# Left-over 64-token blocks of linear attention: two heads on a zero-filled 128x128 block, one full-array product

## The chip, the cores and the metric

The kernel runs on one core of a Trainium2 chip. The metric is the device time of one execution in microseconds (us), as a median over repeated runs. Profiles come from one profiled execution. TensorE is called PE, its weight loads PEld, VectorE DVE, ScalarE ACT, GpSimd POOL, and SyncE SP; SP issues the transfers.

## The reference

Linear attention with random features is followed by two dense feed-forward layers on the same tokens. Everything is float32.

```python
batch, n_heads, seq, head_dim = (4, 8, 576, 64)          # 128 features
q_s, k_s = (q * scale, k * scale)
def phi(x):
    proj = np.einsum('bhsd,md->bhsm', x, omega)           # 64 -> 128
    h = proj - np.sum(x * x, axis=-1, keepdims=True) / 2.0
    return np.exp(h - np.max(h, axis=-1, keepdims=True)) / np.sqrt(m)
kv = np.einsum('bhsm,bhsd->bhmd', phi(k_s), v)
num = np.einsum('bhsm,bhmd->bhsd', phi(q_s), kv)
den = np.einsum('bhsm,bhm->bhs', phi(q_s), np.sum(phi(k_s), axis=2))[..., None] + 1e-06
x = (num / den)                                           # as (2304, 512)
x = leaky(x @ moe_w_in, 0.01) @ moe_w_out                 # 512 -> 2048 -> 512
h = x @ moe2_w_in
out = (h * clip(h + 3, 0, 6) / 6) @ moe2_w_out            # 512 -> 2048 -> 512
```

## The kernel before

Heads are held in pairs: partitions 0 to 63 of a tile are one head's 64 features, partitions 64 to 127 the other's. A sequence of 576 tokens is four blocks of 128 tokens and one left-over block of 64. The function `scores` projects a unit's blocks with `omega` (the tile `wn`, which holds omega twice, once for each half of the partitions). The stationary operand of each product is a token block from the tile `xT`, the moving operand is 64 rows of `wn` with 128 columns. So one product uses half of PE's rows, and two of them, one for each head of the pair, form a couple on the two halves. For a left-over block the 64 tokens of head 0 go to partitions 0 to 63 of a bank and those of head 1 to partitions 64 to 127 of the same bank; such a product uses a quarter of the array, 64 rows by 64 columns. These products stand on line 753 (units of queries and of keys) and on line 774 (`K_tail`: the left-over keys of all four head pairs of a batch at once).

After the products `features` takes minima on DVE (L719), adjusts them (L722, L724), and takes exponentials on ACT (L729). A key unit then multiplies with the values (L822), transposes (L829) and sums keys (L846). A query unit forms its denominators on DVE (L922, reciprocal L928), scales on POOL or DVE (L933), transposes on PE (L948) and multiplies with `kvf` (L979).

`PARTS` cuts each batch's queries into units for five groups of tokens: an entry (group, f, half) has f full blocks and, if half is true, a left-over block. There are three shapes with a left-over block: `half` alone (one unit with four head pairs in batch 0 and one in batch 3), f=1 with half (two units of two head pairs, batch 1), and f=3 with half (four units of one head pair, batch 2).

The first dense layer (`moe1`) runs in products on full-array tiles on lines 502 to 504, three for each float32 product split in a high and a low part. Its weights are unpacked from 64-bit numbers and split on DVE, ACT and POOL (L532 to L552, L486, L487) while it runs, in the first 160 us. The attention of a group is laid among the products of the dense layer of the group before it. The second layer (lines 1076 and 1176) fills the rest of the time.

The order of every engine's work comes from a planner, `Graph.run`, which runs before the kernel is built. It keeps a clock for each engine, takes costs from the code (`"pe", nh * (f + half) * 224.0`), and always issues the operation that can start first. For attention work on PE it has a mode: "S" for products on halves of the rows (scores), "N" for products on halves of the columns (L822, L979), "F" for full-array float32 work, "M" for the dense layers. `WAIT` holds an operation of a mode back if PE last ran "M", so that work of one mode gathers, and `TURN` is the planner's price of a change of mode. So an edit to a cost or a mode can move any attention operation.

Of the kernel before, what the change touches and what calls it, by code (L numbers as in the profile page):

```python
# [19 lines left out]
B, H, S, D = 4, 8, 576, 64  # L20
# [17 lines left out]
PACE = 2.215  # L38
WAIT = {"S": 4500.0, "N": 2000.0, "F": 1500.0}
FOLLOW = 500.0  # L40
# [313 lines left out]
def attn_moe_kernel(ctx: ExitStack, tc: tile.TileContext, qT, kT, qn, kn, v1, om2, w1i, w1o, w2i, w2o, out):  # L354
# [378 lines left out]
    def scores(f, half, xsrc, nsrc, due, nh=1):  # L733

        cols, before = layout(f, half, nh)
        one = f * 128 + 64 * half
        ntok = nh * one
        sq = squares(sum(cols), nsrc, due, nh)
        src = Buf("xT")
        to = lambda: src.tiles[0][:, 0:ntok]  # L740
        g.op(dma((lambda: to().rearrange("p (h t) -> p h t", h=nh)) if nh > 1 else to, xsrc, 128 * ntok * 4), wr=[src], due=due - O2)
        ps = [Ps(g.use) for _ in cols]
        hs = [Buf("h" if c > 1 else "hh") for c in cols]

# [12 lines left out]
        features(ps, hs, cols, before, sq, due, nh)  # L757
        return hs, cols
# [3 lines left out]
    def K_tail(b, due):  # L762
# [3 lines left out]
        last64[b] = h  # L766
        g.op(dma(lambda: src.tiles[0][:, 0:HP * 64].rearrange("p (h t) -> p h t", h=HP), kT[b, :, :, 512:576].rearrange(
            "h p t -> p h t"), 128 * HP * 256), wr=[src], due=due - O2)

        def mm():  # L770
            for hp in range(HP):
                for e in range(2):
                    r = slice(64 * e, 64 * e + 64)
                    nc.tensor.matmul(p.tiles[0][r, hp * 128:hp * 128 + 128], lhsT=src.tiles[0][r, hp * 64:hp * 64 + 64], rhs=wn[r],
                                     start=True, stop=True)
# [123 lines left out]
    def Q_unit(grp, b, hps, f, half, s0, col0, o, due):  # L899
        n, nh = f * 128 + 64 * half, len(hps)  # L900
        ncol, N, F = 2 * f + half, nh * n, f * 128
        if nh == 1:
            xsrc, nsrc = qT[b, hps[0], :, s0:s0 + n], qn[b, hps[0], :, col0:col0 + ncol]
        else:
            h0, h1 = hps[0], hps[-1] + 1
            xsrc = qT[b, h0:h1, :, s0:s0 + n].rearrange("h p t -> p h t")
            nsrc = qn[b, h0:h1, :, col0:col0 + ncol].rearrange("h p c d -> p h c d")
# [373 lines left out]
    for b in range(B):  # L1281
        s0 = col0 = 0
        for i, (grp, f, half) in enumerate(PARTS[b]):
            o = b * S + s0 - GT[grp]
            many_ = min(HP, 4 // max(1, f + half)) if grp else 1
            part = [[("Q", b, list(range(k, k + many_)), f, half, s0, col0, o)] for k in range(0, HP, many_)]
# [4 lines left out]
            s0, col0 = s0 + f * 128 + 64 * half, col0 + 2 * f + half  # L1291
    wi1, wo1 = [], []
# [157 lines left out]
```

## Time and profile before

| | |
|---|---|
| median of 3 runs | 869.18 us (868.69 to 870.06) |
| profiled execution, its own time | 870.25 us |
| span of the profile | 868.4 us |
| PE busy | 855.1 us (98%) |
| DVE busy | 661.5 us (76%) |
| ACT busy | 511.7 us (59%) |
| POOL busy | 197.1 us (23%) |
| transfers | 192.76 MB, mean 222 GB/s |

The span reaches from the first to the last recorded instruction; 1.85 us of the execution lie outside of it. Busy time of PE is that of overlapping products, whose ends are modelled, so the cost of a PE operation is read from the start of one row to the start of the next. A float32 product appears as two records, a transpose as one.

### The profile page before, as it was taken

Reading aid. Unit: us, or ns where it says so; the run is one execution under the profiler, and the core shown is the slowest. Engines: PE = TensorE matmul, PEld = TensorE weight load, DVE = VectorE, ACT = ScalarE, POOL = GpSimd, SP = SyncE. Lnnn points to the kernel's source line nnn. Section 1 sums busy time; section 2 is a strip of 40 time slices with the busy share of each in tenths; the row PEclk is TensorE's granted clock in tenths of the full one; section 3 lists DMA queues with packets and bytes.
Section 4 is the critical chain, followed back from the end, with each engine's and each line's share of the span. In section 5 each row is a group of like instructions: output and inputs, shape, how many; then the busy total and the mean of one; then the engine's idle time right before and its main releaser. Section 6 shows DMA issues by size and latency. Waiting matters only on the chain.

```text
span 868.4 us, 17807 instructions
## 1 busy us (share of the span) xinstructions
PE 855.1 (98%) x6340; PEld 776.5 (89%) x6340; DVE 661.5 (76%) x1714; ACT 511.7 (59%) x1162; POOL 197.1 (23%) x289
## 2 busy tenths in 40 slices
PE   9999999999999999999999999999999999999998
PEld 8988777889877877888888889999999999999997
DVE  6998988966996773666778747796678779868765
ACT  6987887976688654544565445544543454345442
POOL 0124363432314231010101002131002213322110
PEclk9999999999999999999999999999999999999999
DMA  9565654677367504998788718877896784687451
GB/s 334 173 189 184 194 186 141 207 249 219 120 215 251 172 25 161 339 356 331 271 290 319 260 49 301 271 297 248 279 318 216 235 269 136 220 269 246 134 163 45
DMA packets 88616, 192.76 MB, mean 222 GB/s; under 512 B 14416, under 2 KB 40656, under 8 KB 88528
## 3 DMA queue, kind: packets, MB, share of 16 engines
q1 hardware_dynamic: 88528, 191.63, 65.6%
q8 instruction: 50, 0.82, 0.4%
q14 instruction: 38, 0.31, 0.1%
HBM read 147.55 MB, written 44.04 MB: 221 GB/s over the span
## 4 chain that ended last, share of the span: by engine, by line
PE 81%; DVE 12%; DMA 3%; ACT 2%; issue 1%; POOL 0%; SPq 0%; DVEq 0%
PE bank L1076 18%; PE bank L1176 16%; PE bank L502 13%; PE bank L503 12%; PE bank L504 12%; PE bank L753 3%; DVE junk L922 2%; DMA late_w<-in 1%; PE bank L822 1%; PE bank L979 1%; DVE wt L545 1%; DVE wst L542 1%; DVE w L486 1%; DVE nm L719 1%; PE bank L948 1%
## 5 line engine op out<-in xcount | busy, mean ns | idle before, releaser
L483 ACT COPY late_u<-bank 128x256 f32<-128x256 f32 (+1 forms) x100 | 38.4, 384 | 83.8 <-PE bank L1176 70.8
L1018 DVE TENSOR_TENSOR g<-bank,g 128x512 fp32r<-128x512 f32 (+1 forms) x80 | 50.7, 634 | 44.3 <-ACT g L483 43.7
L1076 PE MATMUL bank<-w,g 128*128 128x256 f32 x606 | 80.9, 276 | 0.5 <-DVE g L486 0.5
L1076 PEld LDWEIGHTS bank<-w,g 128*128 128x128 f32 x606 | 74.1, 192 | 0.9 <-DVE g L486 0.7
L1016 ACT ACTIVATE bank<-bank 128x512 f32<-128x512 f32 (+1 forms) x80 | 44.2, 553 | 50.7 <-PE bank L504 50.5
L1176 PE MATMUL bank<-x,late_w 128*128 128x256 f32 x564 | 70.8, 275 | 0.8 <-DMA late_w<-in 0.7
L1176 PE MATMUL bank<-w,late_w 128*128 128x256 f32 x534 | 71.4, 276 | 0.1
L729 ACT ACTIVATE h<-bank,nm 128x128 f32<-128x128 f32 x228 | 64.4, 384 | 6.4 <-DVE nm L724 5.8
L1176 PEld LDWEIGHTS bank<-x,late_w 128*128 128x128 f32 x564 | 67.0, 192 | 1.3 <-DVE late_xr L490 0.9
L502 PE MATMUL bank<-g,w 128*128 128x512 f32 (+1 forms) x180 | 67.4, 375 | 0.2 <-DVE g L1018 0.2
L502 PE MATMUL bank<-x,w 128*128 128x512 f32 (+1 forms) x180 | 66.9, 372 | 0.0
L1176 PEld LDWEIGHTS bank<-w,late_w 128*128 128x128 f32 x534 | 65.6, 192 | 0.6 <-DMA late_w<-in 0.3
L504 PE MATMUL bank<-x,w 128*128 128x512 f32 (+1 forms) x180 | 64.6, 359 | 1.0 <-DVE x L486 1.0
L504 PE MATMUL bank<-g,w 128*128 128x512 f32 (+1 forms) x180 | 64.7, 359 | 0.1
L503 PE MATMUL bank<-x,w 128*128 128x512 f32 (+1 forms) x180 | 64.5, 358 | 0.0
L503 PE MATMUL bank<-g,w 128*128 128x512 f32 (+1 forms) x180 | 64.5, 358 | 0.0
L719 DVE TENSOR_REDUCE nm<-bank 128x4 f32<-128x512 f32 (+2 forms) x76 | 47.5, 653 | 14.7 <-PE bank L753 13.3
L1076 PE MATMUL bank<-second_w,g 128*128 128x256 f32 x423 | 56.6, 275 | 0.0
L933 POOL TENSOR_TENSOR h<-h,den 128x512 f32<-128x512 f32 (+2 forms) x32 | 33.5, 1051 | 85.1 <-DVE den L928 53.8
L1076 PEld LDWEIGHTS bank<-second_w,g 128*128 128x128 f32 x423 | 51.9, 192 | 0.0
L483 ACT COPY u<-bank 128x256 f32<-128x256 f32 (+1 forms) x52 | 21.6, 415 | 43.6 <-PE bank L1176 31.4
L922 DVE CUSTOM_DVE_ANT_0 junk<-h,zr 128x128 bf16<-128x128 f32 (+1 forms) x128 | 44.7, 386 | 1.7 <-ACT h L729 0.7
(388 smaller groups left out, 2365.2 us busy)
## 6 DMA issues: line engine op xcount, KB each, us to landing
late_w<-in SPq DMA_DIRECT2D x85, 512.0 KB, 4.6
in<-late_w SPq DMA_DIRECT2D x32, 512.0 KB, 5.2
late_w<-in SPq DMA_DIRECT2D x39, 256.0 KB, 4.8
third_w<-in SPq DMA_DIRECT2D x19, 512.0 KB, 4.7
wst<-w2i SPq DMA_DIRECT2D x16, 512.0 KB, 4.4
wst<-w2o SPq DMA_DIRECT2D x16, 512.0 KB, 4.9
x_t<-late_w SPq DMA_DIRECT2D x12, 512.0 KB, 4.9
v<-v SPq DMA_DIRECT2D x14, 330.0 KB, 4.0
```

The source lines that it names most:

```text
L483: return [("act", c_act(n, psum), lambda: nc.scalar.copy(dst(), src())), dve if psum else dve + (True,)]
L502: nc.tensor.matmul(o, lhsT=ah, rhs=bh, start=start, stop=False)
L503: nc.tensor.matmul(o, lhsT=al, rhs=bh, start=False, stop=False)
L504: nc.tensor.matmul(o, lhsT=ah, rhs=bl, start=False, stop=stop)
L719: g.op([("dve", c_dve(c * 128), lambda raw=raw, n_=n_: nc.vector.tensor_reduce(out=n_()[:, :, 0], in_=raw(), axis=AX.X, op=ALU.min))], rd= ...
L729: nc.scalar.activation(h.tiles[0][:, q * 128:q * 128 + 128], raw()[:, q], AF.Exp, bias=nm.tiles[0][:, q], scale=-1.0)
L922: nc.vector.tensor_tensor_reduce(out=jk.tiles[0][r, q % 2], in0=h.tiles[0][r, q * 128:q * 128 + 128], in1=zr[k].tiles[0][r, e], scale=1.0, ...
L933: eng.tensor_tensor(out=x, in0=x, in1=den.tiles[1][:, 0:c].to_broadcast([128, c, 128]), op=ALU.mult)
L1016: g.op([("act", c_act(n, True), lambda: nc.scalar.activation(P(), P(), AF.Prelu, alpha=0.01))], wr=[p], due=d)
L1018: g.op([("dve", c_dve(n), lambda: nc.vector.tensor_tensor(out=G1(), in0=P(), in1=G0().bitcast(F32), op=ALU.subtract))], rd=[p, (gg, 0)], w ...
L1076: nc.tensor.matmul(acc[bank].tiles[0][:, half * 256:half * 256 + 256], lhsT=src.tiles[x][:, q * 128:q * 128 + 128], rhs=woven(w[k].tiles[y ...
L1176: nc.tensor.matmul(R[r](), lhsT=w[x], rhs=m[y], start=start and k == n == 0, stop=k == 1 and n == 2, skip_group_check=True)
```

## The change

Left-over blocks of two heads are laid out as one 128x128 block: the 64 tokens of head 0 take the first 64 columns on partitions 0 to 63, those of head 1 the last 64 columns on partitions 64 to 127, and the other two quarters are zeros. The host fills in the zeros, so `qT` and `kT` have 640 columns instead of 576. One product with all 128 rows of `wn` then gives the same bank contents as the two products before. `scores` issues these full-array products first and then the couples on halves; for `half` alone the unit has no couple left and its mode is "F". `K_tail` does the same for batches 1, 2 and 3; batch 0 keeps its two products. The left-over blocks cost 112 instead of 224 in the planner, and the wait for mode "F" is 1100 instead of 1500. Line numbers of the changed kernel after `K_tail` are 5 higher.

```diff
-WAIT = {"S": 4500.0, "N": 2000.0, "F": 1500.0}
+WAIT = {"S": 4500.0, "N": 2000.0, "F": 1100.0}
...
-        one = f * 128 + 64 * half
+        one = (f + half) * 128
...
         def mm():
+            for k in range(nh if half else 0):
+                at = (k * (f + 1) + f) * 128
+                nc.tensor.matmul(ps[0].tiles[0][:, at:at + 128], lhsT=src.tiles[0][:, at:at + 128], rhs=wn, start=True, stop=True)
             for k in range(nh):
-                for i in range(f + half):
-                    n = 128 if i < f else 64
+                for i in range(f):
                     for e in range(2):
                         r = slice(64 * e, 64 * e + 64)
-                        bank, o = (e, slice(0, 128)) if i < f else (0, r)
-                        at = (k * f + i if bank else k * (f + half) + i) * 128
-                        nc.tensor.matmul(ps[bank].tiles[0][o, at:at + 128], lhsT=src.tiles[0][r, k * one + i * 128:k * one + i * 128 + n],
+                        at = (k * f + i if e else k * (f + half) + i) * 128
+                        nc.tensor.matmul(ps[e].tiles[0][:, at:at + 128], lhsT=src.tiles[0][r, k * one + i * 128:k * one + i * 128 + 128],
                                          rhs=wn[r], start=True, stop=True)
-        g.op([("pe", nh * (f + half) * 224.0, mm)], rd=[src], wr=ps, also=hs, due=due, mode="S")
+        g.op([("pe", nh * (f * 224.0 + half * 112.0), mm)], rd=[src], wr=ps, also=hs, due=due, mode="S" if f else "F")
...
+        w = 128 if b else 64
...
             for hp in range(HP):
+                c = slice(hp * 128, hp * 128 + 128)
+                if b:
+                    nc.tensor.matmul(p.tiles[0][:, c], lhsT=src.tiles[0][:, c], rhs=wn, start=True, stop=True)
+                    continue
...
-        g.op([("pe", HP * 224.0, mm)], rd=[src], wr=[p], also=[h], due=due, mode="S")
+        g.op([("pe", HP * (112.0 if b else 224.0), mm)], rd=[src], wr=[p], also=[h], due=due, mode="F" if b else "S")
...
-            xsrc, nsrc = qT[b, hps[0], :, s0:s0 + n], qn[b, hps[0], :, col0:col0 + ncol]
+            xsrc, nsrc = qT[b, hps[0], :, s0:s0 + (f + half) * 128], qn[b, hps[0], :, col0:col0 + ncol]
...
+                if half:
+                    for e in range(2):
+                        at = c + e * (64 if b else first)
+                        y[b, :, 64 * e:64 * e + 64, at:at + 64] = x[b, :, e, :, s:s + 64]
+                    c, s = c + 128, s + 64
```

On PE the two left-over units that stand next to each other just ahead of the first dense products (a `half` unit of queries of batch 0, then `K_tail` of batch 1; `x8` counts products) read like this before:

```order
L892 MATMUL bank_182<-ident,u_0_117 128x128 x4
L753 MATMUL bank_177<-wn,xT_0_140 64x128 x8
L774 MATMUL bank_178<-wn,xT_0_141 64x128 x8
L502 MATMUL bank_176<-x_101,w_85 128x512
L503 MATMUL bank_176<-x_101,w_85 128x512
```

And now:

```order
L897 MATMUL bank_182<-ident,u_0_117 128x128 x4
L748 MATMUL bank_177<-wn,xT_0_140 128x128 x4
L776 MATMUL bank_178<-wn,xT_0_141 128x128 x4
L502 MATMUL bank_176<-x_101,w_85 128x512
L503 MATMUL bank_176<-x_101,w_85 128x512
```

Sixteen products on quarters became eight on the full array, in the same place. Up to here the order of PE has not moved.

The second unit with f=1 and a left-over block stands on PE before as follows; the rows left out repeat the three of its first head pair, then finish the product with the values, and bring 26 blocks (three rows each) of the dense layer's products, a key unit's L829 and L846 and a query unit's six products, up to the unit's transposes of `h_0_146`:

```order
L504 MATMUL bank_179<-g_106,second_w_3_0_1066 128x512
L753 MATMUL bank_176<-wn,xT_0_141 128x128
L753 MATMUL bank_181<-wn,xT_0_141 128x128
L753 MATMUL bank_176<-wn,xT_0_141 64x128 x2
...
L822 MATMUL bank_178<-h_0_149,v_0_144 64x128
...
L829 MATMUL bank_178<-ident,kvf_0_129 128x128
...
L846 MATMUL bank_178<-zr_0_135,ones 128x256
...
L948 MATMUL bank_181<-ident,h_0_146 128x128
```

And now, where the rows left out are one repeat, the rest of 12 blocks of dense products, and a query unit's six products with one block:

```order
L504 MATMUL bank_178<-x_103,second_w_8_0_1061 128x512
...
L748 MATMUL bank_181<-wn,xT_0_141 128x128 x2
L754 MATMUL bank_181<-wn,xT_0_141 128x128
L754 MATMUL bank_183<-wn,xT_0_141 128x128
...
L502 MATMUL bank_180<-g_105,second_w_7_0_1060 128x512
...
L754 MATMUL bank_178<-wn,xT_0_140 128x128
...
L504 MATMUL bank_180<-g_107,third_w_0_0_1617 128x512
L953 MATMUL bank_183<-ident,h_0_146 128x128
```

The unit moved behind the key unit's work, and less of PE's work lies between its products and its transposes.

On DVE, between the same unit's first minimum (L719) and its last reciprocal (L928, now L933), stand besides its own small rows these rows of other work before:

```order
L719 TENSOR_REDUCE nm_0_123<-bank_176 128x4
...
L545 SCALAR_TENSOR_TENSOR stage_wt_0_0_1079<-stage_wt_0_0_1079,wst_0_109 128x512
...
L1018 TENSOR_TENSOR g_105<-bank_183,g_105 128x512
L486 TENSOR_TENSOR second_w_8_0_1071<-stage_wt_1_0_1080,second_w_8_0_1071 128x512
L486 TENSOR_TENSOR second_w_7_0_1070<-stage_wt_0_0_1079,second_w_7_0_1070 128x512
L542 SCALAR_TENSOR_TENSOR wst_0_108<-wt_0_110,wst_0_108 128x512
...
L545 SCALAR_TENSOR_TENSOR wt_0_110<-wt_0_110,wst_0_108 128x512
...
L697 TENSOR_REDUCE sq_0_125<-xn_0_142 128x6
L928 RECIPROCAL den_1_189<-den_0_188 128x2
```

And now:

```order
L719 TENSOR_REDUCE nm_0_123<-bank_181 128x4
L1023 TENSOR_TENSOR g_106<-bank_178,g_106 128x512
...
L545 SCALAR_TENSOR_TENSOR wt_0_110<-wt_0_110,wst_0_109 128x512
...
L534 TENSOR_SCALAR wt_0_111<-wst_0_108 128x512
...
L697 TENSOR_REDUCE sq_0_125<-xn_0_142 128x6
...
L542 SCALAR_TENSOR_TENSOR wst_0_108<-wt_0_111,wst_0_108 128x512
...
L933 RECIPROCAL den_1_189<-den_0_188 128x2
```

The two weight splits (L486) have left this stretch, and one of the two L545 became an L534.

From the end of attention on, at about 335 us, PE's rows stand in the same order in both kernels.

## Rows read from the trace of the kernel before

**Rows 1.** Windows: stretch, length, busy us (instructions) per engine, clock, DMA share, GB/s.

```profile
core 0: us, PE busy (x) PEld busy (x) DVE busy (x) ACT busy (x) POOL busy (x), PEclk, DMA share, GB/s
45.00:160.00 115.00, 110.71 (x696) 90.19 (x696) 105.16 (x251) 90.22 (x202) 48.19 (x58) 1.00 0.55 173
160.00:335.00 175.00, 173.59 (x1362) 143.67 (x1361) 130.57 (x438) 126.23 (x341) 55.05 (x76) 1.00 0.56 177
335.00:840.00 505.00, 503.40 (x3692) 479.09 (x3691) 374.90 (x878) 248.79 (x496) 88.66 (x140) 1.00 0.74 254
```

**Rows 2.** Chain that ended last, by line: 45 to 160 us, then 160 to 335.

```profile
by line: DVE wt L545 8.6%; DVE junk L922 8.5%; DVE wst L542 7.7%; DVE w L486 7.2%; DMA stage_wst<-w1i 6.9%; DVE nm L719 5.6%; DVE g L1018 5.0%; issue 4.8%; PE bank L503 4.6%; PE bank L502 4.1%; PE bank L504 4.0%; DVE second_w L486 2.6%; DVE
...
by line: PE bank L502 21.4%; PE bank L504 18.6%; PE bank L503 18.6%; PE bank L753 10.8%; PE bank L979 6.1%; PE bank L822 5.6%; PE bank L948 4.9%; DVE junk L922 2.8%; PE bank L846 2.2%; DVE nm L719 1.0%; ACT h L729 1.0%; PE bank L829 0.8%; D
```

**Rows 3.** Timeline of PE, two left-over units: start, busy, instruction, records.

```profile
46.38 1.09 PE L753 MATMUL bank<-wn,xT 64*64 64x128 f32 x16
47.30 1.04 PE L774 MATMUL bank<-wn,xT 64*64 64x128 f32 x16
48.27 0.48 PE L502 MATMUL bank<-x,w 128*128 128x512 f32 x1
```

**Rows 4.** Timeline of PE, `K_tail` of batch 2.

```profile
168.64 1.09 PE L774 MATMUL bank<-wn,xT 64*64 64x128 f32 x16
169.66 0.87 PE L948 MATMUL bank<-ident,h 128*128 128x128 f32 x6
```

**Rows 5.** Timeline of PE, a key unit's eight products between dense products.

```profile
74.97 1.16 PE L753 MATMUL bank<-wn,xT 64*128 64x128 f32 x16
76.06 0.48 PE L502 MATMUL bank<-x,w 128*128 128x512 f32 x1
76.38 0.38 PE L503 MATMUL bank<-x,w 128*128 128x512 f32 x1
76.59 0.38 PE L504 MATMUL bank<-x,w 128*128 128x512 f32 x1
```

**Rows 6.** Timeline of PE, second unit with f=1 and a left-over block.

```profile
125.16 0.38 PE L504 MATMUL bank<-g,second_w 128*128 128x512 f32 x1
125.47 1.65 PE L753 MATMUL bank<-wn,xT 64*128 64x128 f32 x16
127.05 1.09 PE L822 MATMUL bank<-h,v 128*64 128x128 f32 x16
```

**Rows 7.** Timeline of PE, a unit with f=3 and a left-over block.

```profile
217.17 1.30 PE L753 MATMUL bank<-wn,xT 64*128 64x128 f32 x16
218.41 0.38 PE L502 MATMUL bank<-g,second_w 128*128 128x256 f32 x1
```

**Rows 8.** Timeline of PE, one full-array float32 product of 256 columns.

```profile
72.50 0.59 PE L846 MATMUL bank<-zr,ones 128*128 128x256 f32 x2
72.74 0.57 PE L502 MATMUL bank<-g,w 128*128 128x512 f32 x1
73.15 0.38 PE L503 MATMUL bank<-g,w 128*128 128x512 f32 x1
```

**Rows 9.** Timeline of PE, two full-array float32 products of 128 columns.

```profile
17.08 0.71 PE L811 MATMUL bank<-ident,kvf 128*128 128x128 f32 x4
17.62 1.91 PE L874 MATMUL bank<-kvf,first_tq 128*128 128x66 f32 x16
```

**Rows 10.** Timeline of POOL, scaling of two query units, with waits.

```profile
137.59 1.71 POOL L933 TENSOR_TENSOR h<-h,den 128x512 f32<-128x512 f32 x2 [5.41 <-ACT bank L1016]
...
152.74 0.83 POOL L933 TENSOR_TENSOR h<-h,den 128x384 f32<-128x384 f32 x1 [0.74 <-DVE den L928]
```

**Rows 11.** Timeline of PE, first row behind a unit of three couples.

```profile
140.26 0.44 PE L948 MATMUL bank<-ident,h 128*128 128x128 f32 x2
```

**Rows 12.** Groups of DVE by form: busy us, mean ns, idle before.

```profile
L486 DVE TENSOR_TENSOR second_w<-wt,second_w 128x512 fp32r<-128x512 f32 x4 | 2.6, 680 | 0.0
```

**Rows 13.** DMA issues: count, KB each, median us to landing.

```profile
xT<-kT SPq DMA_DIRECT2D x13, 256.0 KB, 4.5
...
xT<-kT SPq DMA_DIRECT2D x3, 128.0 KB, 3.3
```

More of the change, by code (lines that the diff above doesn't have):

```diff
@@ L766, in K_tail @@
         last64[b] = h
-        g.op(dma(lambda: src.tiles[0][:, 0:HP * 64].rearrange("p (h t) -> p h t", h=HP), kT[b, :, :, 512:576].rearrange(
-            "h p t -> p h t"), 128 * HP * 256), wr=[src], due=due - O2)
+        w = 128 if b else 64
+        g.op(dma(lambda: src.tiles[0][:, 0:HP * w].rearrange("p (h t) -> p h t", h=HP), kT[b, :, :, 512:512 + w].rearrange(
+            "h p t -> p h t"), 128 * HP * w * 4), wr=[src], due=due - O2)
         def mm():
             for hp in range(HP):
+                c = slice(hp * 128, hp * 128 + 128)
+                if b:
+                    nc.tensor.matmul(p.tiles[0][:, c], lhsT=src.tiles[0][:, c], rhs=wn, start=True, stop=True)
+                    continue
                 for e in range(2):
                     r = slice(64 * e, 64 * e + 64)
-                    nc.tensor.matmul(p.tiles[0][r, hp * 128:hp * 128 + 128], lhsT=src.tiles[0][r, hp * 64:hp * 64 + 64], rhs=wn[r],
-                                     start=True, stop=True)
-        g.op([("pe", HP * 224.0, mm)], rd=[src], wr=[p], also=[h], due=due, mode="S")
+                    nc.tensor.matmul(p.tiles[0][r, c], lhsT=src.tiles[0][r, hp * 64:hp * 64 + 64], rhs=wn[r], start=True, stop=True)
+        g.op([("pe", HP * (112.0 if b else 224.0), mm)], rd=[src], wr=[p], also=[h], due=due, mode="F" if b else "S")
         features([p], [h], [HP], [0], sq, due)
@@ L902, in Q_unit @@
         if nh == 1:
-            xsrc, nsrc = qT[b, hps[0], :, s0:s0 + n], qn[b, hps[0], :, col0:col0 + ncol]
+            xsrc, nsrc = qT[b, hps[0], :, s0:s0 + (f + half) * 128], qn[b, hps[0], :, col0:col0 + ncol]
         else:
             h0, h1 = hps[0], hps[-1] + 1
-            xsrc = qT[b, h0:h1, :, s0:s0 + n].rearrange("h p t -> p h t")
+            xsrc = qT[b, h0:h1, :, s0:s0 + (f + half) * 128].rearrange("h p t -> p h t")
             nsrc = qn[b, h0:h1, :, col0:col0 + ncol].rearrange("h p c d -> p h c d")
@@ L1281, in attn_moe_kernel @@
     for b in range(B):
-        s0 = col0 = 0
+        s0 = col0 = wide0 = 0
         for i, (grp, f, half) in enumerate(PARTS[b]):
@@ L1285, in attn_moe_kernel @@
             many_ = min(HP, 4 // max(1, f + half)) if grp else 1
-            part = [[("Q", b, list(range(k, k + many_)), f, half, s0, col0, o)] for k in range(0, HP, many_)]
+            part = [[("Q", b, list(range(k, k + many_)), f, half, wide0, col0, o)] for k in range(0, HP, many_)]
             if i == 0:
@@ L1290, in attn_moe_kernel @@
             units[grp] += part
-            s0, col0 = s0 + f * 128 + 64 * half, col0 + 2 * f + half
+            s0, col0, wide0 = s0 + f * 128 + 64 * half, col0 + 2 * f + half, wide0 + (f + half) * 128
     wi1, wo1 = [], []
@@ L1385, with by_row @@
     from concourse.bass_utils import run_bass_kernel_spmd
-    def by_row(x):
-        return x.reshape(B, HP, 2, S, D).transpose(0, 1, 2, 4, 3).reshape(B, HP, 2 * D, S)
+    def by_row(x, parts, first=64):
+        y = np.zeros((B, HP, 128, 640), x.dtype)
+        x = x.reshape(B, HP, 2, S, D).transpose(0, 1, 2, 4, 3)
+        for b in range(B):
+            c = s = 0
+            for f, half in parts[b]:
+                y[b, :, :, c:c + f * 128] = x[b, :, :, :, s:s + f * 128].reshape(HP, 128, f * 128)
+                c, s = c + f * 128, s + f * 128
+                if half:
[3 more added lines that the diff above has]
+                    c, s = c + 128, s + 64
+        return y
     def by_token(x, parts):
@@ L1429 @@
     arrays = {
-        "qT": by_row(q),
-        "kT": by_row(k),
+        "qT": by_row(q, [[p[1:] for p in x] for x in PARTS]),
+        "kT": by_row(k, [[(4, True)]] * B, 0),
         "qn": by_token(q, [[p[1:] for p in x] for x in PARTS]),
```

## Prediction

> **What bounds the kernel now.** I read the windows first. From 45 to 160 us PE is busy 110.71 of 115 us, so 4.29 us are idle, and DVE is busy 105.16 us, 91% [rows 1]. From 160 to 335 us PE is idle 1.41 us and DVE has room, 131 of 175 us [rows 1]. From 335 to 840 us PE is idle 1.60 of 505 us [rows 1]. So PE is the engine that runs out of time almost everywhere, and time taken from it before 335 us should reach the end. The chain of work that ended last says where this is less sure: between 45 and 160 us most of its large shares are DVE's (weight unpacking L545 and L542, splits L486, denominators L922), with 4 to 5% for each of PE's lines, while between 160 and 335 us PE's lines 502 to 504 alone hold 59% [rows 2]. In the first stretch PE and DVE are nearly level. A microsecond saved on PE there can come back as a wait for DVE.
>
> **The change part by part.**
>
> *Units that are left-over blocks only.* There are five: queries of batches 0 and 3, and `K_tail` of batches 1, 2 and 3. Each has eight products on quarters of the array. Start to start they take 0.92 and 0.97 us [rows 3] and 1.02 us [rows 4]; I take 0.97. Each becomes four full-array float32 products of 128 columns. No such product between dense ones stands in the trace. From below: one of 256 columns and the dense product behind it take 72.50 to 73.15, 0.65 us; less 0.215 for a dense product of 512 columns (76.38 to 76.59 [rows 5]) that is 0.435, so 0.215 for 128 columns [rows 8]. From above: two of 128 columns with different weights take 0.54 us, 0.27 each [rows 9], and this pair stands behind products on halves, so a change of mode may be in it. I take 0.215, for the row without that change. Five units: 5 x (0.97 - 0.86) = 0.55 us.
>
> *Two units with f=1.* Each alternates two couples on halves with two couples on quarters and takes 1.58 us [rows 6], where four couples on halves take 1.09 us [rows 5]. It becomes two full products and two couples: 0.43 + 0.545 = 0.975. Two units: 1.21 us.
>
> *Four units with f=3.* Now 1.24 us [rows 7], one of four shown. Three couples at 0.2725 and one full product: 0.82 + 0.215 = 1.03. Four units: 0.83 us.
>
> *Changes of mode.* Into products on halves PE takes 0.31 us from a dense product's start instead of 0.215 [rows 6], and behind them the first dense product takes 0.32 instead of 0.215 [rows 5]: 0.20 us for each stretch of products on part of the array. Around full-array float32 work I see no such price: the 0.435 above already holds its way in and out [rows 8]. In the order of PE there are 54 such stretches before and 50 now; two went because the two units at 46 us and `K_tail` of batch 2 are full-array work now, two because the planner put neighbours together. 4 x 0.20 = 0.80 us.
>
> One rule speaks against full-array products. The row: 256 columns in two records cost 0.435 us in all [rows 8]. The Trainium skill, page "TensorE: Matmul & The Clock Gate", section on packing small matmuls (The mechanism), says that a weight load overlaps a running product only when it goes to another row group; two full-array products share all row groups, so by it their loads could not hide. If each record's load took as long as the record, a product would cost about 0.43 instead of 0.215, 28 of them 6.0 us more, and the saving above would turn into a loss. The trace does not agree: 0.435 us for two records of 256 columns leaves no room for two loads in the open, and 0.27 is the most that a 128-column product shows [rows 9].
>
> *Transfers.* 28 left-over blocks are fetched with 128 columns instead of 64, 32 KB more each, 0.9 MB in all, 4 us of transfer at the kernel's mean of 222 GB/s, spread over some 280 us in which the DMA share is 0.55 [rows 1]. A fetch of 128 KB lands after 3.3 us, one of 256 KB after 4.5 us [rows 13]; both are planned 12 us ahead of their products (`due - O2`, O2 being 12 us). I cost this at nothing, under that lead. Without it a unit would start 1.2 us late, five times 6 us at most.
>
> *The planner.* It counts 0.112 us for a product that I put at 0.215, so it believes PE up to 2.9 us further ahead than it will be; operations then stand a little late for DVE, never early. The order moves much from 50 to 335 us. Where PE now comes sooner to work that DVE prepares, a wait can grow. Two places look tight. The second f=1 unit ends its products at 127.05 [rows 6] and is scaled on POOL at 139.30 [rows 10]: 12.25 us. Now PE has 12 dense blocks of 0.65 us (three products of 0.215), a query unit's three couples (0.82 + 0.20) and one more block between products and transposes: 9.5 us. But two weight splits of 0.68 us [rows 12] left DVE's queue in that stretch, so it needs about 10.9: 1.4 us short. The next unit, with three couples, ends its products at 140.26 [rows 11] and is scaled at 153.57 [rows 10], 13.3 us; DVE's rows from first minimum to last reciprocal go from 31 to 23, so about 9.9 us (estimate in proportion), against some 9.2 us of PE work: 0.7 short. Together 2.1 us of new waiting. It replaces part of the 4.29 us already idle there [rows 1], since the same DVE queue serves both; I take 0.7 us as the net, with 0 and 2.1 as ends. Queued behind a waiting transpose is all of PE; PE's queue is in order.
>
> Sum: 0.55 + 1.21 + 0.83 + 0.80 = 3.4 us of PE work, less 0.7 of waiting, 2.7 us. The profiled execution took 870.25 us (span 868.4 and 1.85 around it); 870.25 - 2.7 = 867.55. That execution lies 1.07 us above the median of the runs, 869.18, so against the median I forecast 866.5 us. What a measurement of this kernel can tell from no change is about 0.2%, 1.74 us.
>
> **The rivals.**
>
> *DVE keeps the first stretch.* Everything saved ahead of 160 us is lost in waits for DVE: 0.17 from the two units at 46 us, 1.21 from the f=1 units and about 0.4 of mode changes, 1.8 us. What stays is 1.6 less some 0.6 of waiting: 869.18 - 1.0 = 868.2. For it speaks DVE's 91% and the chain [rows 1, 2]; against it, that DVE has less ahead of the last weights than before: its last weight split (L486) ahead of 160 us stands 27 rows earlier (row 330 instead of 357), POOL having taken one over.
>
> *Transposes wait for the scores' vector work (slower).* If DVE takes the two tight units as long as before, the first is 2.75 us late (12.25 against 9.5) and the second 4.1 us (13.3 against 9.2), 6.8 us on PE with nothing in its place. 869.18 - 3.4 + 6.8 = 872.6. It decides for slower from 5.1 us of new waiting on. Against it: the rows that left DVE's queue between the two ends; for it: PE comes sooner and DVE is nearly full.
>
> *The waits shrink.* DVE reaches the last weights sooner, and half of the 4.29 us idle on PE goes as well: 869.18 - 3.4 - 2.1 = 863.7. For it speaks the order of DVE; against it the two tight units.
>
> *Full-array products cost 0.27* [rows 9]: 28 x 0.055 = 1.5 us more, 868.0 with the same waits.
>
> *Weight loads of full-array products lie open.* Load and product of a record take turns, 0.43 us a product: 28 x 0.215 = 6.0 us more, 866.5 + 6.0 = 872.5. It is the case that the page's rule above would give; [rows 8, 9] speak against it.
>
> **How the numbers follow.** Chances: the forecast 0.40, DVE keeps the first stretch 0.20, transposes wait 0.14, waits shrink 0.14, products at 0.27 us 0.09, loads open 0.03. The likeliest gives 866.5 us; its own range is 865.1 (no new waiting, 3.4 saved, and 0.7 of old waits gone) to 867.9 (2.1 of new waiting). The range for 8 in 10 reaches from 863.3 (just past the shrunk waits) to 870.9 and leaves out the two slow cases and a little below. Faster by over 0.2% is below 867.44: most of the first case, all of the shrunk waits, a little of the others, 0.57. Slower is above 870.92: 0.17. The rest, 0.26, is no change.
>
> **What would show it.** Right: `K_tail` and `half` units as rows 128*128 with 0.11 us a record, 0.86 us for four products, and the next dense product at the usual 0.215; f=1 units of 0.98 us and f=3 units of 1.03 us from start to start; PE's idle time between 45 and 160 us within 1 us of 4.29; the first product on line 1181 (L1176 before) some 2.7 us sooner in the span. Wrong: idle time before transposes (L953), released by POOL or DVE at L938 or L933, of several us; idle time before dense products released by L486; rows of 0.13 us or more a record at L748 and L776. The prediction fails most easily in the waits, since a small shift in a planned order moves all of them, and they are as large as the saving.

## Result and the profile after

The changed kernel took 873.03 us (median of 7 runs, 871.84 to 876.29) against 869.44 us for the kernel before on the same chip: ratio 1.0052, 95% interval 1.0039 to 1.0066. It is slower by 3.6 us, where 866.5 was forecast. The span of the profiled execution is 871.3 us.

The windows after, in the columns of [rows 1]:

```profile
45.00:160.00 115.00, 110.02 (x672) 91.46 (x672) 101.69 (x247) 91.55 (x203) 49.46 (x56) 1.00 0.54 173
160.00:335.00 175.00, 170.91 (x1325) 141.97 (x1322) 131.26 (x451) 121.96 (x334) 54.26 (x75) 1.00 0.57 182
335.00:840.00 505.00, 503.46 (x3680) 478.57 (x3679) 375.20 (x874) 246.07 (x491) 95.05 (x141) 1.00 0.73 253
```

Against [rows 1], PE's idle time from 45 to 160 us grew from 4.29 to 4.98 us, from 160 to 335 us from 1.41 to 4.09; behind 335 it is as it was. Together 9.07 us of idle time from 45 to 335 us instead of 5.70.

The products themselves, in PE's timeline after:

```profile
46.64 1.06 PE L748 MATMUL bank<-wn,xT 128*128 128x128 f32 x8
...
48.34 0.46 PE L502 MATMUL bank<-x,w 128*128 128x512 f32 x1
...
136.46 0.61 PE L748 MATMUL bank<-wn,xT 128*128 128x128 f32 x4
137.00 0.72 PE L754 MATMUL bank<-wn,xT 64*128 64x128 f32 x8
137.64 0.48 PE L502 MATMUL bank<-g,second_w 128*128 128x512 f32 x1
...
169.27 1.10 PE L776 MATMUL bank<-wn,xT 128*128 128x128 f32 x8
170.13 0.36 PE L502 MATMUL bank<-g,w 128*128 128x256 f32 x1
```

Four full-array products take 0.86 us from start to start (169.27 to 170.13), where eight on quarters took 1.02 [rows 4]; the two units at 46 us take 1.70 together instead of 1.89 [rows 3]. A unit with f=1 takes 1.18 us from its first product (136.46) to the next dense one (137.64); its first half, two full products, takes 0.54. So the operation that was changed is faster, as forecast, and what is lost lies in waits. PE's waits after, the longest first:

```profile
engine line waited for: us in total, times, longest us
PE bank L851 <- POOL zr L847: 2.5, 1, 2.5
PE bank L504 <- DVE g L1023: 2.3, 2, 1.5
PE bank L504 <- DVE x L486: 1.5, 3, 0.6
```

The third is hardly new. Before, PE waits as long for splits on L486:

```profile
PE bank L504 <- DVE x L486: 1.0, 1, 1.0
...
PE bank L503 <- DVE third_w L486: 0.5, 2, 0.2
```

None of the three stands in the place where I looked. Each is one or a few places in the timeline. The longest, on PE:

```profile
74.00 0.70 PE L851 MATMUL bank<-zr,ones 128*128 128x256 f32 x2 [2.52 <-POOL zr L847]
...
303.61 0.48 PE L504 MATMUL bank<-g,w 128*128 128x512 f32 x1 [1.48 <-DVE g L1023]
```

What POOL did ahead of 74 us, and what it did while DVE worked towards the product that ends the wait at 303.61:

```profile
67.96 0.62 POOL L552 CAST w<-first_wt 128x512 fp32r<-128x512 f32 x1 [4.74 <-DVE first_wt L545]
68.54 2.31 POOL L491 TENSOR_TENSOR h<-h 128x256 f32<-128x256 f32 x2
70.81 1.76 POOL L491 TENSOR_TENSOR zr<-h 128x128 f32<-128x128 f32 x2
72.53 1.42 POOL L847 TENSOR_TENSOR zr<-zr,ht 64x128 f32<-64x128 f32 x2
...
300.64 2.16 POOL L938 TENSOR_TENSOR h<-h,den 128x512 f32<-128x512 f32 x2 [6.34 <-ACT h L729]
```

And DVE's rows at the second place:

```profile
300.57 0.28 DVE L927 CUSTOM_DVE_ANT_0 junk<-h,zr 128x128 bf16<-128x128 f32 x1
...
300.78 1.12 DVE L927 CUSTOM_DVE_ANT_0 junk<-h,zr 128x128 bf16<-128x128 f32 x1
...
301.83 1.11 DVE L927 CUSTOM_DVE_ANT_0 junk<-h,zr 128x128 bf16<-128x128 f32 x1
...
302.88 0.68 DVE L1023 TENSOR_TENSOR g<-bank,g 128x512 fp32r<-128x512 f32 x1
```

The same places before: the key unit's products with the values on PE and its first sums on POOL, then two of DVE's rows at the second place:

```profile
66.27 1.09 PE L822 MATMUL bank<-h,v 128*64 128x128 f32 x16
...
67.07 2.39 POOL L491 TENSOR_TENSOR h<-h 128x256 f32<-128x256 f32 x2 [1.47 <-PE bank L822]
```

```profile
300.16 0.69 DVE L1018 TENSOR_TENSOR g<-bank,g 128x512 fp32r<-128x512 f32 x1
...
302.23 1.12 DVE L922 CUSTOM_DVE_ANT_0 junk<-h,zr 128x128 bf16<-128x128 f32 x1
```

The first wait: before, POOL is idle and starts the sums 0.80 us after the unit's first product with the values (66.27 to 67.07). Now the last weight cast (L552) ahead of the sums in POOL's queue waits 4.74 us for DVE, and the sums start 3.21 us after that product (65.33 on L827, to 68.54), 2.4 us later than before; PE waits 2.52. That the cast is to blame is read from these rows; no run moved it alone. The second: two denominators (L927) take 1.1 us instead of 0.28 while POOL scales two blocks, and the product of `g` (L1023) that PE waits for stands behind them. The slow denominators are not new, one of the two of 1.12 us before is shown; what is new is the order, for before a product of `g` (L1018 at 300.16) stands ahead of them, and PE does not wait.

The first product of the second layer (line 1176 before, 1181 after) starts at 488.58 us instead of 486.20; from it to the last recorded wait for a split (836.20, 838.76) both kernels take 350 us. The start is 2.4 us later: 3.4 us more of idle time as above, and 0.8 more ahead of 45 us, at the first fetches of blocks, where executions with the same fetches differ nearly as much (no wait in `e6_minus24` below, 0.69 us in `e7_minus95`), less what the products save.

### The profile page after: what moved, and what is told of

Same layout as the page of the kernel before. It is cut to its first block, busy times and chain, and to the rows that moved or that the text cites. A ratio compares the mean times of both kernels' runs of the same rounds, so it can differ in the third digit from the quotient of the medians.

```text
span 871.3 us, 17698 instructions
## 1 busy us (share of the span) xinstructions
PE 853.6 (98%) x6284; PEld 777.6 (89%) x6284; DVE 660.9 (76%) x1723; ACT 506.9 (58%) x1153; POOL 204.7 (23%) x289
## 4 chain that ended last, share of the span: by engine, by line
PE 75%; DVE 5%; DMA 3%; issue 1%; ACT 0%; POOL 0%; DVEq 0%; SPq 0%; ACTq 0%
PE bank L1081 17%; PE bank L1181 16%; PE bank L502 12%; PE bank L504 12%; PE bank L503 11%; PE bank L754 2%; DMA late_w<-in 2%; PE bank L984 1%; DVE junk L927 1%; PE bank L827 1%; PE bank L953 1%; DVE nm L719 1%; DMA wst<-w2i 1%; DVE g L486 1%; DVE g L1023 0%
## 5 line engine op out<-in xcount | busy, mean ns | idle before, releaser
L1023 DVE TENSOR_TENSOR g<-bank,g 128x512 fp32r<-128x512 f32 (+1 forms) x80 | 50.6, 634 | 35.9 <-ACT g L483 35.2
L504 PE MATMUL bank<-x,w 128*128 128x512 f32 (+1 forms) x180 | 64.8, 360 | 1.5 <-DVE x L486 1.5
L504 PE MATMUL bank<-g,w 128*128 128x512 f32 (+1 forms) x180 | 64.7, 359 | 1.5 <-DVE g L1023 1.5
L719 DVE TENSOR_REDUCE nm<-bank 128x4 f32<-128x512 f32 (+2 forms) x76 | 47.4, 655 | 16.0 <-PE bank L754 14.0
L938 POOL TENSOR_TENSOR h<-h,den 128x512 f32<-128x512 f32 (+2 forms) x32 | 34.6, 1083 | 72.2 <-DVE den L933 37.0
L927 DVE CUSTOM_DVE_ANT_0 junk<-h,zr 128x128 bf16<-128x128 f32 (+1 forms) x128 | 43.6, 379 | 0.7
```

The costliest lines, as they stand in the source:

```text
L504: nc.tensor.matmul(o, lhsT=ah, rhs=bl, start=False, stop=stop)
L719: g.op([("dve", c_dve(c * 128), lambda raw=raw, n_=n_: nc.vector.tensor_reduce(out=n_()[:, :, 0], in_=raw(), axis=AX.X, op=ALU.min))], rd= ...
L927: nc.vector.tensor_tensor_reduce(out=jk.tiles[0][r, q % 2], in0=h.tiles[0][r, q * 128:q * 128 + 128], in1=zr[k].tiles[0][r, e], scale=1.0, ...
L938: eng.tensor_tensor(out=x, in0=x, in1=den.tiles[1][:, 0:c].to_broadcast([128, c, 128]), op=ALU.mult)
L1023: g.op([("dve", c_dve(n), lambda: nc.vector.tensor_tensor(out=G1(), in0=P(), in1=G0().bitcast(F32), op=ALU.subtract))], rd=[p, (gg, 0)], w ...
```

## The experiments

Two questions were asked: does the order or the products lose the time, and where does the products' saving go. "Idle" is PE's idle time from 45 to 335 us (290 less the two windows' busy times; 5.70 before, 9.07 after); "start" is the first product of the second layer.

**Products and order apart.** `e1_old_plan`: the changed products with the planner's old numbers, so that the order is the old one.

```diff
-WAIT = {"S": 4500.0, "N": 2000.0, "F": 1100.0}
+WAIT = {"S": 4500.0, "N": 2000.0, "F": 1500.0}
-        g.op([("pe", nh * (f * 224.0 + half * 112.0), mm)], ..., mode="S" if f else "F")
+        g.op([("pe", nh * (f + half) * 224.0, mm)], ..., mode="S")
```

(and likewise in `K_tail` and the planned sizes of the two transfers). `e2_new_plan_only` is the reverse: the products of before on quarters, with the planner's new numbers.

> The left-over blocks as full-array products, with the planner's costs, modes, waits and transfer sizes of before, so that every engine's order is that of before. Theory A (the products save what was forecast, the loss is waits that the new order made): 2.3 to 3.0 us under before, ratio 0.9965 to 0.9975; the tail rows cost 0.86 to 0.94 us and recorded idle time of PE from 45 to 335 us stays at 5 to 6 us. Rival B (the full-array products themselves, or the wider transfers, cost the time): 2 to 4 us over before, ratio 1.002 to 1.005. Rival C (DVE sets the first stretch, so savings of PE turn into waits): within 1 us of before.

> The kernel before with nothing but the changed kernel's numbers in the planner (cost 112, mode F, wait 1100, sizes of the transfers): its order, with the old products on quarters. Theory A: the waits of the new order without the saving of the products, 873.0 plus 2.3, 875 us, ratio 1.006 to 1.008. Rival B: the order is innocent, 868 to 870 us, ratio 0.998 to 1.001. Rival C: the same waits, partly filled by the longer products, 873 to 874 us.

In brackets behind each ratio stands its 95% interval. e1: 869.93 us against 869.06, ratio 1.0009 (0.9997 to 1.0021), idle 5.60, start 483.71. e2: 877.59, ratio 1.0095 (1.0081 to 1.0110), idle 9.93, start 493.25, with the waits of the changed kernel:

```profile
PE bank L846 <- POOL zr L842: 2.5, 1, 2.5
PE bank L504 <- DVE g L1018: 2.3, 2, 1.5
PE bank L753 <- ACT h L729: 1.6, 3, 0.6
PE bank L504 <- DVE x L486: 1.4, 3, 0.6
```

With no new product in it, the order alone costs 0.95%, 8.3 us; within that order the full-array products give some 3.7 back (1.0052 against 1.0095). So the loss is the order's. But e1, without that loss, gains nothing either: its time is in the range of rival C, though its second layer starts 2.5 us sooner, which C does not have.

The 8.3 us are more than e2's idle time explains (9.93 us against 5.70). In e2's profile, PE's granted clock falls to 0.50, 1.2 instead of 2.4 GHz, just behind the wait of 2.52 us. Windows of e2 and of the changed kernel behind that wait, in the columns of [rows 1], then rows of e2:

```profile
73.95:77.30 3.35, 3.35 (x9) 2.69 (x8) 1.29 (x2) 2.62 (x5) 0.00 (x0) 0.50 0.96 337
...
74.05:77.40 3.35, 3.35 (x16) 2.70 (x18) 1.29 (x2) 2.63 (x5) 0.00 (x0) 1.00 0.93 314
```

```profile
75.24 0.63 PE L502 MATMUL bank<-g,w 128*128 128x512 f32 x1
75.67 0.63 PE L503 MATMUL bank<-g,w 128*128 128x512 f32 x1
```

Eight dense products in a row take 0.21 us longer each (0.43 in these rows instead of 0.215), so the wait costs 1.7 us more than its own length. The same wait in the profile of the changed kernel passes without it (1.00). The profiles of e3, e4 and `e12_wait1200` below show such a fall too; none in the old order does while PE has products left.

**The planner's numbers.** `e3_wait1500` is the changed kernel with `"F": 1500.0`; `e4_cost215` has `half * 215.0` and `215.0 if b else 224.0`, the cost that a product really has.

> The changed kernel with the wait for mode F at 1500 as before; the order differs from both. Theory A, in which the loss is an accident of one order: another order has another sum of waits, anywhere from 865 to 874 us, and its recorded idle time of PE explains its time within 1 us. Rival B: 872 to 874 us like the change, since the products are the same. Rival D (the cost of 112 in the planner, half of what a product takes, makes all such orders bad): 872 us or more.

> The changed kernel with 215 instead of 112 as the planner's cost of a full-array product, which is what the trace shows (0.215 us). Rival D (the planner's wrong cost makes the waits): 866 to 868 us. Theory A without D (an accident of one order): anywhere from 865 to 874 us, explained by its idle time within 1 us. Rival B: 872 to 874 us.

e3: 883.65 us, ratio 1.0161 (1.0147 to 1.0176), idle 13.93. It misses theory A, which had 874 us at most and a time explained by idle time within 1 us: idle time grew by 8.2 us, the time by 14.6. In its profile the clock is at 0.50 twice, from 107.2 us on, behind waits of 1.8 us in all, and from 240.3 us on, behind one of 2.49; some 3 us come of that, the rest is open. e4: 872.16, ratio 1.0036 (1.0021 to 1.0050), idle 9.39, with the clock at 0.50 from 302.7 us on, behind a wait of 2.12 us: the true cost does not bring a much better order, and rival D is out.

**Does time ahead of the second layer reach the end?** In the kernel before, its order unchanged, the third product (L504) of some dense blocks just behind 340 us is left out (`e6_minus24` 11 of them, `e7_minus95` 44) or made twice (`e8_plus24`, 11).

```diff
+        short = 380 < next(calls) <= 391
...
-        nc.tensor.matmul(o, lhsT=ah, rhs=bl, start=False, stop=stop)
+        if not short:
+            nc.tensor.matmul(o, lhsT=ah, rhs=bl, start=False, stop=stop)
```

> The kernel before, in unchanged order, with 11 products less on PE (the third product, L504, of 11 dense blocks of the first layer just after 340 us; their low halves are left out of the sum): 11 x 0.215 = 2.4 us of PE work less in a stretch where PE has no idle time and DVE has room. This asks whether a saving that is there at the start of the second layer reaches the end. Theory 'stream' (the second layer's weights come at their own pace, by DMA, and hold PE back when it is early): the first product of the second layer comes 2.4 us sooner, the end less than 1.2 us sooner, ratio 0.9987 to 1.0005, with idle time on PE behind 486 us grown by 1.5 us or more, released by DMA. Rival 'PE alone' (what the old order with full-array products lost behind 486 us was its own bad luck): the end is 2.4 us sooner too, ratio 0.9973.

> As the run with 11 products less, but 44 of them: 9.5 us of PE work less just after 340 us. Theory 'stream': most of it is given back, the end is at most 4.7 us sooner, ratio 0.9945 or more, and waits for DMA (late_w, third_w) on PE behind 400 us grow by 4 us or more. Rival 'PE alone': 9.5 us sooner at the end, ratio 0.989.

> The kernel before, in unchanged order, with 11 products more (L504 of 11 dense blocks just after 340 us is made twice; the low halves are added twice): 2.4 us of PE work more. Theory 'stream', if the stream is the bound in the kernel before as well: PE being later finds its weights there, the 0.7 us wait for late_w at 767 us goes, and the end is less than 1.7 us later, ratio below 1.002. If PE and the stream are level in the kernel before, and rival 'PE alone': 2.4 us later, ratio 1.0027. With the run of 11 products less it says whether gains and losses ahead of the second layer count alike.

e6: 867.87 us against 869.6, ratio 0.9983 (0.9972 to 0.9995): between the two theories. e7: 864.50, ratio 0.9945 (0.9929 to 0.9960): 4.8 of 9.5 us arrive, as 'stream' had it, but the waits for a weight fetch recorded behind 480 us are 1.5 us, not 4; some of the loss lies ahead of the second layer, which starts 7.5 us sooner (478.72), 1.4 of it by chance ahead of 335 us: DVE and ACT hold PE up 2.4 us on the way. e8: 873.22, ratio 1.0040 (1.0024 to 1.0056). The loss arrives in full (3.5 us by the ratio for 2.4 put in, where 'stream' had less than 1.7), the large saving by half. A wait of e7 on PE, for a weight fetch (`late_w` and `third_w` hold weights of the second layer):

```profile
532.16 1.60 PE L1180 MATMUL bank<-w,late_w 128*128 128x256 f32 x12 [1.11 <-DMA late_w<-in]
```

These traces also show that one program's executions differ: with the same order ahead of 335 us, idle is 4.06 us in e6, 5.51 in e8, 5.70 before (its wait of 1.18 us for ACT at 88 us is 0.37 in e8 and gone in e6). The 9.07 after is well outside.

**One wait taken away.** `e9_no_sums` is the changed kernel without the two sums L491 at 68.54.

```diff
...
+                if i:
+                    alts = [a[:2] + ((lambda f=a[2]: next(sums) > 2 and f()),) + a[3:] for a in alts]
```

> The changed kernel in its own order, with two of POOL's sums left out (the two 128x256 sums, L491, of the first key unit whose sums POOL makes, at 68.5 us; that pair of heads' key sum then holds half of the tokens): 2.3 us less of POOL work ahead of the 2.52 us wait of L851 at 74 us, the longest new wait. Theory 'each wait counts by itself': PE is about 2.2 us sooner behind 75 us, and the first product of the second layer is still about 2 us sooner than in the changed kernel, 486.5. Rival 'the next in line': PE then waits as long a few us later, for DVE's weights or for the next sums, and the first product of the second layer comes within 0.7 us of 488.6.

871.63 us, ratio 1.0026 (1.0014 to 1.0038). Its timeline of PE, rows that answer to 74.00, 303.61 and 488.58 after:

```profile
72.29 0.70 PE L854 MATMUL bank<-zr,ones 128*128 128x256 f32 x2 [0.61 <-POOL zr L850]
...
301.92 0.48 PE L504 MATMUL bank<-g,w 128*128 128x512 f32 x1 [1.48 <-DVE g L1026]
...
486.89 1.50 PE L1184 MATMUL bank<-w,late_w 128*128 128x256 f32 x12
```

The lead of 1.7 us at 72 us is 1.69 at 302 and 1.69 at 487, and the wait at 302 is as long as ever. This wait counts by itself; the others were not taken away.

**The old order again, and other orders.** `e10_old_plan_again` is e1 once more. `e11_wait1000` and `e12_wait1200` are the changed kernel with `"F": 1000.0` and `1200.0`; `e13_before_wait1400` is the kernel before with `"F": 1400.0`.

> The full-array products in the order of the kernel before, once more, for a second profiled execution. In the first, PE reached the second layer 2.5 us sooner than in the kernel before and gave 3.3 us back behind it, in an order that is the same there; the kernel with 11 products less reached it 3.35 us sooner and gave back 0.25. Theory 'chance of one execution': this time the second layer takes what it takes in the kernel before (350.0 us from its first product to the wait of the last split, within 1 us) and the span is 866.5 or less; the median of all runs of the two calls is then still a mixture, ratio 0.998 to 1.001. Rival 'early loses': the second layer takes 352 us or more again, with waits for third_w, late_w near 568, 623 and 638 us, and the span is 868.5 or more.

> The changed kernel with the planner's number WAIT F at 1000 instead of 1100: the same products, another order. Theory 'the order decides' (each order has waits of its own, as large as the saving or larger, and none of them follows from the full-array products): the time moves by 1.5 us or more to either side of 873.0, and the sum of PE's recorded waits from 45 to 335 us moves with it. Rival 'the products decide' (what was lost lies in the full-array products themselves, whatever the order): 872 to 874.

> The changed kernel with the planner's number WAIT F at 1200 instead of 1100: the same products, another order again. Theory 'the order decides': 1.5 us or more to either side of 873.0, together with PE's recorded waits from 45 to 335 us. Rival 'the products decide': 872 to 874.

> The kernel before with the planner's number WAIT F at 1400 instead of 1500: its own products on quarters of the array, another order. Theory 'the order decides': 1.5 us or more slower than 869.4 (the order of the kernel before has less waiting than its neighbours), with no full-array product in it. Rival 'the products decide': within 1 us of 869.4.

Against 869.05: e10 869.22 us, ratio 1.0000 (0.9985 to 1.0015), start 483.75; e11 870.44, 1.0022 (1.0006 to 1.0038), idle 5.53; e12 874.23, 1.0053 (1.0038 to 1.0068), idle 6.73; e13 871.02, 1.0020 (1.0011 to 1.0029), idle 6.36. e11, with the products of the changed kernel, is 2.6 us faster than it; e13, with those of the kernel before, is 2.0 slower than that: the order decides in both. Where e13 loses its time its profile does not show: its second layer starts at 485.53, 0.67 us sooner than before, and takes 352.5 us instead of 350.0 in the same order of PE. e12 misses: it is level with the changed kernel by ratio (1.0053 against 1.0052), its smaller idle time ahead of 335 us being lost to 2.2 us of waits for late_w and to the clock, which is at 0.50 from 74.6 us on, behind the wait of 2.52 us (eight dense products at 0.43 us again, 1.7 us). In e11 the clock parts the executions: the five of its ten with a mean granted clock of 0.999 or more took 868.48 to 870.41 us, the five with less 870.47 to 873.67. None of the executions in the old order has less than 0.999. e10's second layer has lost its long waits; in e1 and e10, PE's waits over 0.3 us between 560 and 770 us are:

```profile
568.35 0.91 PE L1181 MATMUL bank<-x,third_w 128*128 128x256 f32 x6 [0.52 <-DMA third_w<-in]
623.09 1.58 PE L1181 MATMUL bank<-x,late_w 128*128 128x256 f32 x12 [1.02 <-DVE u L1192]
638.35 1.91 PE L1181 MATMUL bank<-x,late_w 128*128 128x256 f32 x15 [0.95 <-DVE u L1192]
```

```profile
765.63 1.58 PE L1181 MATMUL bank<-x,late_w 128*128 128x256 f32 x12 [0.70 <-DMA late_w<-in]
```

The same instructions in the same order wait in one execution and not in the next, so the length of these waits is not set by the order alone. (The DVE row named at 623.09 cannot be it: in the kernel before the same product starts without a wait, ahead of that DVE row.) The spans are 869.2 and 866.5.

**The fetches halved.** `e15_before_half_fetch` is the kernel before, `e16_old_plan_half_fetch` is e1, both with half of each fetch of the second layer's first weights.

```diff
+        m = n // 2 if kind == "in" else n
...
-            b.tiles[2]...[:, :, to:to + n].bitcast(F32), d[:, :, cols].bitcast(F32)))],
+            b.tiles[2]...[:, :, to:to + m].bitcast(F32), d[:, :, cols.start:cols.start + m].bitcast(F32)))],
```

> The kernel before with half the bytes of each fetch of the second layer's first weights ('in', line 672: half of the columns are fetched, the other half of each tile keeps what stood there, so the output is not the reference's); order and all else unchanged. The ground for the next run. Recorded waits for late_w and third_w on PE go (0.7 us in the profile of before); 868.0 to 869.0, and nearer to 867.5 if the runs without a profile wait longer than the profiled one.

> The full-array products in the order of the kernel before, with the same halved fetches. Theory 'stream' (the second layer's weight fetches take the saving): without them in the way the saving shows, this is 1.7 us or more faster than the kernel before with halved fetches, and its trace has no wait for late_w or third_w over 0.4 us. Rival 'elsewhere' (something other than the fetches takes it): within 0.8 us of the kernel before with halved fetches.

The kernel before took 869.27 here. e15 took 866.61 us, ratio 0.9966 (0.9954 to 0.9979); e16 865.82 us, 0.9959 (0.9946 to 0.9973). Two things come of it. First, by the medians the fetches cost the kernel before 2.7 us, more than was expected (the interval is 1.8 to 4.0), of which its profile records 0.7 as waits. The two profiles show less: the second layer takes 348.4 us in e15 instead of 350.0, so 1.6 us; e15's other 2.05 us of lead are there at 335 us, before the first such fetch is issued at 473 us, 1.4 of them at the wait at 88 us named above, which is gone in e15. Second, the new products gain 0.8 us here, not 2.5: theory 'stream' is not borne out in its size, and the result stands at the edge of rival 'elsewhere'. With the same order the two traces can be laid side by side, e15 first, then e16:

```profile
47.89 0.48 PE L502 MATMUL bank<-x,w 128*128 128x512 f32 x1
...
484.15 1.50 PE L1177 MATMUL bank<-w,late_w 128*128 128x256 f32 x12
...
832.56 1.83 PE L1077 MATMUL bank<-w,g 128*128 128x256 f32 x14 [0.50 <-DVE g L486]
```

```profile
47.50 0.46 PE L502 MATMUL bank<-x,w 128*128 128x512 f32 x1
...
53.68 0.48 PE L504 MATMUL bank<-g,w 128*128 128x512 f32 x1 [0.32 <-DVE g L1024]
...
89.40 0.70 PE L852 MATMUL bank<-zr,ones 128*128 128x256 f32 x2 [0.62 <-POOL zr L848]
...
482.78 1.50 PE L1182 MATMUL bank<-w,late_w 128*128 128x256 f32 x12
...
515.80 0.94 PE L1182 MATMUL bank<-x,late_w 128*128 128x256 f32 x6 [0.37 <-DMA x<-x_t]
...
831.82 1.83 PE L1082 MATMUL bank<-w,g 128*128 128x256 f32 x14 [0.50 <-DVE g L486]
```

From one shared dense product to the next, e16 gains 0.29 us at the two units at 46 us, about 0.4 and 0.49 at the f=1 units, 0.28 at `K_tail` of batch 2, 0.27 at that of batch 3 and the f=3 unit beside it, 0.13 at the last left-over unit and 0.04 to 0.22 at each other f=3 unit, some 2.3 us. New waits (0.32 and 0.62 in the rows, 0.26 more at 243 us) take about 1 us, so that 1.37 arrive at 482.78; a load of 512 KB (x_t), which was not halved, takes 0.6 at 515.80, and 0.74 arrive at the end.

**The longest wait mended.** `e14_wait1000_sums_dve` is e11 with the two sums L491 of its longest wait (2.1 us, L851 again) made on DVE; all work is done.

```diff
...
+                if i:
+                    dve, pool = alts[0][2], alts[1][2]
+                    alts[1] = ("pool", alts[1][1], lambda dve=dve, pool=pool: dve() if next(sums) < 3 else pool())
```

> The changed kernel with WAIT F at 1000, and two of POOL's sums (the 128x256 sums, L491, at 68.8 us) made on DVE instead, at the same place in the order: all work is done. POOL has 2.3 us less ahead of the 2.1 us wait for its sums at 74 us, DVE some 0.8 us more just ahead of its own 2.5 us wait at 75.9 us. Theory 'each wait counts by itself': PE is 1.3 to 2.0 us sooner behind 75 us and at the second layer (484.9 before), and the median 868.4 to 869.5, level with or just under the kernel before (869.05), ratio 0.999 to 1.0005. Rival 'the next in line' (DVE's part then releases the same product, or the weights behind it come later): within 0.6 us of 870.4, ratio 1.0015 or more.

868.11 us against 869.27, ratio 0.9990 (0.9978 to 1.0001), idle 3.56, start 483.52 instead of e11's 484.88: the wait is gone, and 1.4 of its 2.1 us reach the second layer. It is the best version with the new products, level with the kernel before or 0.1% under it.

## Why the prediction was wrong

*Costs of the products: right in the main.* Rows of 0.11 us a record and 0.86 us for four are as forecast, and loads in the open, the rival at 872.5, did not come. The sum of 3.4 us was too large: with the order unchanged about 2.3 us were measured (e15 to e16), where 3.0 were forecast, since two of the four changes of mode, 0.40 us, go only in the new order. The f=1 units gave about 0.45 instead of 0.605 each, the f=3 units mostly less than their 0.21; after, a unit with f=1 takes 1.18 us to the next dense product, where 0.98 was forecast: its two full products take 0.54 instead of 0.43, its two couples 0.64 instead of 0.545. That a change of mode inside the unit, which I left out of that 0.975, takes the difference is likely but not shown by itself.

*Transfers at nothing: right.* Behind 45 us no product waits for a block's fetch; the waits for blocks after, 0.73 us at 7.42 us and 0.45 at 9.04, are at the first fetches, and traces with the old layout have such waits too (0.69 us in e7).

*"less 0.7 of new waiting": the step that failed.* The idle time from 45 to 335 us grew by 3.4 us. Of the two tight places neither shows: no wait of L953 for POOL's L938 stands among the long ones. "Operations then stand a little late for DVE, never early" was the wrong picture. I looked for waits where DVE's queue had grown shorter between two ends that I had chosen, and did not look at POOL's queue, where sums that start 2.4 us late behind a waiting cast cost PE 2.5 us (e9: 1.7 of it, to the second layer), nor for products of `g` that moved behind denominators on DVE (1.5 us at 303.61). Idle time ahead of dense products released by L486, which I named as a sign of being wrong, did not come: it is 1.5 us in the list above, as it was before. The forecast also had no price for PE's clock, which was at its lower level behind such waits in four profiles: in e2 that made 1.7 us more, and of the 7 runs of the changed kernel two, 875.00 and 876.29 us, have a mean granted clock of 0.997. The slower rival had the right side and nearly the right size (872.6) by another mechanism, which is luck.

*"Time taken from it before 335 us should reach the end": half right.* PE's 1.60 us of idle time in 505 [rows 1] looked like a stretch that only PE sets. e15 shows fetches in it, 1.6 us by the profiles and 2.7 by the medians, e7 that half of a large saving is lost behind 340 us. What takes the rest of the saving in e1 and e10 (0.8 with halved fetches, 0 within 1.3 us with whole ones) is shown in part only: waits in the first layer and one load in e16's trace; that the whole fetches take the last 0.8 fits both results, but lies within their intervals.

*Why the new order is bad, and others less so,* is settled place by place, not as a rule: e3, e11, e12 and e13 show orders from 870 to 884 us for one number changed, and e13 that a neighbour of the old order is slower than it with the old products.

## What to carry to other kernels

Where a planner sets the order, test an edit first in the old order: the edit's gain and the new order's luck are then apart, and here the order lost 8.3 us where the edit took 2.3 us of work from PE, of which 0.8 at most reached the end. To forecast a new order, walk every in-order queue that feeds the bottleneck, the little-used engine's too, and ask of each instruction that moved ahead what it waits for and who stands behind it. Count a wait of the bottleneck by what follows it too: look at PE's granted clock behind each long one. A bottleneck that shows 99% busy may still be paced by transfers: halve their bytes, and see.

## What was not expected of the hardware

DVE's rows are longer here while POOL works on two-operand instructions: L927 takes 1.1 us instead of 0.28 beside L938 (rows above), L922 1.12 beside L933 before. In e11, DVE's rows go from 0.73 to 1.22 us as soon as POOL's sums run (68.82 to 71.09):

```profile
66.84 0.73 DVE L542 SCALAR_TENSOR_TENSOR wst<-wt,wst 128x512 uint32<-128x512 uint32 x1
...
70.46 1.22 DVE L542 SCALAR_TENSOR_TENSOR wst<-wt,wst 128x512 uint32<-128x512 uint32 x1
```

That is read from rows that lie side by side; no run here took POOL's part away at 303 us. PE's clock fell to its lower level behind waits of 1.8 to 2.5 us in e2, e3, e4 and e12, and in the profile of the changed kernel did not behind one of 2.52, so a wait of the same length costs more in one execution than in another. Where the spread between executions of one program comes from, 2.8 us in 15 runs of the kernel before, is open: with half the bytes of the fetches the 5 runs of e15 lie within 0.85 us, but the 4 runs of e3, with whole fetches, lie within 0.50.
